# Two parallel branches on one core: the keys' weights turned by DMA in two halves from two queues, the first token tiles on one queue, and a new order of steps

## The chip, the cores and the metric

The kernel runs on one core of a Trainium2 chip. The metric is the device time of one execution in microseconds. The core has a TensorE (PE) for matmuls, a VectorE (DVE), a ScalarE (ACT), a GpSimd (POOL) and a SyncE (SP); each works through its own instructions in their order. DMAs are issued here from SP and from ACT, so a DMA that ACT issues stands in one queue with ACT's arithmetic.

## The reference

x has 2048 tokens of 512 numbers, all in bf16. Both branches read the same normalised tokens; A is a linear attention with 32 heads of 16, B a dense layer with a mish activation.

```python
xn = _layernorm(x, axis=-1)
return x + _A_ref(xn, A_wqkv, A_w_phi, A_wo) + _B_ref(xn, B_w1, B_b1, B_w2)

# _A_ref: q, k, v from x @ wqkv, 32 heads of 16
pq = jnp.einsum("bhsd,hdf->bhsf", q, w_phi)
pk = jnp.einsum("bhsd,hdf->bhsf", k, w_phi)
phi_q = jnp.concatenate([_softmax(pq, axis=-1), _softmax(-pq, axis=-1)], axis=-1)
phi_k = jnp.concatenate([_softmax(pk, axis=-1), _softmax(-pk, axis=-1)], axis=-1)
kv = jnp.einsum("bhsf,bhsd->bhfd", phi_k, v)
z  = jnp.einsum("bhsf->bhf", phi_k)
num = jnp.einsum("bhqf,bhfd->bhqd", phi_q, kv)
den = jnp.einsum("bhqf,bhf->bhq", phi_q, z)[..., None] + 1e-6
o = num / den                      # then @ wo

# _B_ref: w1 is 512 x 1792, w2 is 1792 x 512
h = jnp.einsum("bsd,df->bsf", x, w1) + b1
sp = jnp.log1p(jnp.exp(-jnp.abs(h))) + jnp.where(h > 0, h, jnp.zeros_like(h))
act = h * jnp.tanh(sp)
return jnp.einsum("bsf,fd->bsd", act, w2)
```

## The kernel before

The tokens lie in 16 tiles of 128 (four groups of four). `STEPS` is a string that lists the steps of the whole kernel in the order in which they are written into the program; `run` (L603) maps each name to a function, and the loop at L623 calls them one by one. Under `manual_schedule` (L128) that order is the order on each engine. The number behind `@` is the PSUM bank (six of them), `v` or `a` at the end puts a copy or an inversion on VectorE or ScalarE. The kernel writes no waits; the tile framework places them from what reads and writes what.

**Ahead of the steps** (L483 to L516) the first loads are issued. SP: token tile 0 (L483), then the transposing DMA of the keys' weights (L143), then tiles 2 and 3 (L489), wv (L490), the first half of w1 (L491), tiles 4 to 7 (L492), the second half of w1 (L493). ACT: wsrc (w_phi, L486), token tile 1 (L487), the bias b1b (L488), and the load of the activation table (L495). TensorE does `WARM` matmuls on constants.

**The keys' weights.** The keys are only used through w_phi, so the product of the two weight matrices is formed once: `load_turned` reads a 512 x 512 part of wqkv transposed into wT (partition = column within a block of 128, then block j, then row). `weights_by_block` (WB, L524) lays w_phi out as a block diagonal Wbd. `fold` (F0, L156) multiplies for one block kt of 128 rows of wqkv the four blocks j: its left operand is `wT[:, j, kt * P : (kt + 1) * P]`, so folds 0 and 1 use rows 0 to 255 and folds 2 and 3 rows 256 to 511. `unfold` (FD, L165) copies each to wkp. The same for the queries is done later (WT, F, FC).

**The first tiles** are normalised one by one: LS (moments, DVE, L170 and L172), RS (the root, POOL, L176 and L177), AZ (L181, DVE), TP (turned by TensorE, L560), TC (copied to xnT, L565). `first_logits` (LP, L209) multiplies tiles 0 and 1 by wkp in one step; L, V and WL (L194) do single tiles, LC and VC (L252, L218) copy them out of PSUM. From tile 4 on, LN does the moments of a group, and AP normalises two tiles and turns them by a transposing DMA from SP (L186). DX and DW load tokens and the weights wo and w2 from SP.

**The rest.** H (L228) and M (L239) are the 56 pieces of B's first layer with the mish. For the eight groups of logits (four of keys, four of queries), E takes the extremes (DVE), X the exponentials (ACT), S the sums (DVE, L305), R and N invert and multiply for keys, A adds up kv on TensorE (L387); KV masks it; W weighs the queries and turns them by DMA (L295); Q is the attention (L418), G copies it out, C divides and turns it by DMA (L458); O is B's second layer (L463), P the projection with wo into the same bank (L470), Y adds the tokens and stores (L477, L478). The last tile is split into 384 and 128 columns (OH, PH, YH).

Of the kernel before, what the change touches and what calls it, by code (L numbers as in the profile page):

```python
# [34 lines left out]
@3; H 23 @1; R 0 0 v; N 0 1; M 21; N 0 0; H 24 @4; M 22; LC 2 3 a; F 0 @5; F 1 @0; E 1 0; E 1 1; M
23; M 24; F 2 @2; E 2 0; E 2 1; FC 0 a; H 25 @3; H 26 @1; FC 1 a; H 27 @4; M 25; M 26; L 3 2 @5; FC
2 a; M 27; V 7 @0; L 3 3 @3; V 11 @1; F 3 @2; L 3 0 @4; LC 3 0 v; LC 3 2 a; L 3 1 @5; A 0 0; X 1 0;
X 1 1; A 0 1; LC 3 3 a; FC 3 v; S 1 0; V 8 @4; LC 3 1 a; VC 7 a; L 4 0 @2; E 3 0; VC 8 a; LC 4 0 a;
L 4 1 @3; LC 4 1 a; L 4 3 @5; VC 11 a; L 4 2 @0; X 2 0; V 9 @4; L 5 0 @2; H 28 @3; H 29 @1; VC 9 a;
LC 4 2 v; M 28; M 29; H 30 @0; H 31 @4; H 32 @3; M 30; H 33 @1; H 34 @0; M 31; M 32; M 33; M 34; H  # L40
35 @4; M 35; H 36 @3; M 36; S 1 1; LC 4 3 a; R 1 0 v; E 3 1; LC 5 0 a; N 1 0; R 1 1 v; H 37 @1; H 38
@0; H 39 @4; H 40 @3; H 41 @5; H 42 @2; S 2 0; A 1 0; M 37; N 1 1; M 38; M 39; M 40; A 1 1; M 41; M
42; X 3 0; L 6 3 @1; L 5 2 @0; V 10 @4; VC 10 a; L 5 1 @3; LC 5 2 a; L 6 0 @5; E 4 0; E 4 1; X 2 1;
S 3 0; V 15 @2; VC 15 a; V 13 @4; VC 13 a; LC 6 0 a; R 2 0 a; S 2 1; DW 3; R 3 0 a; X 3 1; L 6 1 @0;
LC 5 1 a; DW 2; N 3 0; N 2 0; L 5 3 @2; O 0 @4; S 3 1; V 12 @5; V 14 @3; LC 6 1 a; LC 5 3 a; O 1 @0;
L 6 2 @2; R 2 1 a; N 2 1; VC 14 a; LC 6 3 a; VC 12 v; R 3 1 a; N 3 1; X 4 0; A 2 0; S 4 0; LC 6 2 a;
A 2 1; A 3 0; W 4 0 v; X 4 1; H 43 @3; M 43; A 3 1; H 44 @1; H 45 @5; M 44; H 46 @2; M 45; H 47 @3;
M 46; M 47; H 48 @1; KV; H 49 @5; H 50 @2; Q 0 0; M 48; M 49; G 0 0; M 50; H 51 @3; H 52 @1; H 53
@5; S 4 1; W 4 1 v; M 51; M 52; H 54 @2; H 55 @3; Q 0 1; M 53; E 5 0; E 5 1; M 54; E 6 0; L 7 0 @1;
M 55; G 0 1; C 0 a; X 5 0; LC 7 0 a; L 7 1 @5; X 5 1; O 2 @2; O 3 @3; LC 7 1 a; L 7 2 @1; LC 7 2 a;  # L50
S 5 0; Q 1 0; L 7 3 @5; G 1 0; E 6 1; W 5 0 a; P 0; P 1; Y 0; Q 1 1; O 4 @1; G 1 1; LC 7 3 a; O 5
@4; S 5 1; Q 2 0; O 6 @5; C 1 a; P 2; G 2 0; W 5 1 v; Y 1; Q 2 1; P 3; O 7 @0; E 7 0; X 6 0; S 6 0;
G 2 1; Q 3 0; C 2 a; G 3 0; Y 2; Y 3; X 6 1; O 8 @2; Q 3 1; W 6 0 v; E 7 1; S 6 1; P 4; P 5; G 3 1;
C 3 a; Q 4 0; X 7 0; Y 4; W 6 1 v; X 7 1; S 7 0; O 9 @3; O 10 @1; G 4 0; Q 4 1; P 6; P 7; G 4 1; Y
# [8 lines left out]
def kernel(  # L63
# [76 lines left out]
    def load_turned(base_col):  # L140

        wT = lnp.tile([P, 4, 512], BF16, name="wT", tag="xn")
        nc.sync.dma_start_transpose(out=wT[:], in_=A_wqkv[:, base_col : base_col + D])  # L143
        return wT
# [57 lines left out]
    def first_logits(how, *b):  # L202
        for i in range(2):
            pl_of[0, i] = bank(b[i], "pl")[:]
        pairs = [(i, kt) for kt in range(KT) for i in range(2)]
        if how == "t":
            pairs.sort()
        for i, kt in pairs:
            nc.tensor.matmul(  # L209
                pl_of[0, i], lhsT=xnT[:, i, kt, :], rhs=wkp[:, kt, :],  # L210
                start=(kt == 0), stop=(kt == KT - 1),
            )
# [270 lines left out]
    nc.sync.dma_start(x_sb[:, 0, :], x_v[:, 0, :])  # L483
# [172 lines left out]
```

## Time and profile before

| what | us |
|---|---|
| runs: median (lowest to highest) of 3 | 174.08 (173.59 to 174.09) |
| the profiled execution, its own time | 174.0 |
| its span, first to last instruction | 172.3 |
| busy: POOL | 9.4 |
| first fold (L156) starts | 6.65 |
| last matmul ends | 169.65 |
| DMA moved in all | 18.02 MB |

The page gives busy times by engine, the span in 40 slices, DMA queues, the chain of work that ended last (each step is followed back to what released it) and groups of instructions by line; a timeline gives start and length of each instruction, with what ended the idle time before it. Times in it count from the start of the span. A matmul's length includes its way through the array, so that a row of matmuls is best read by their distance: in the chain the 48 of L228 that start at 13.78 us take 10.36 us in all, 0.216 us each, though a single one is shown with 379 ns.

### The profile page before, as it was taken

The page shows a single profiled execution, that of the slowest core. Times are in us where ns is not written, and L with a number is a line of the kernel's source. Part 1 is how long each engine was busy: PE and PEld are TensorE (multiplying, and loading weights), DVE is VectorE, ACT ScalarE, POOL GpSimd, SP SyncE. Part 2 cuts the span into 40 slices and gives each one's busy share as a digit, 9 for nine tenths or more (in the row PEclk, how much of TensorE's full clock was granted, in tenths as well). Part 3 has the DMA queues.
Part 4 walks back from the last instruction along what each step waited for, and adds up shares of the span by engine and source line. Part 5 has one row for each costly group of instructions (what it writes and reads, how often), then busy time and mean ns, then how long its engine had stood idle before and what let it go on. Part 6 is the DMA issues. An engine that isn't in the chain of part 4 may idle for free.

```text
span 172.3 us, 2713 instructions
## 1 busy us (share of the span) xinstructions
PE 168.7 (98%) x1039; PEld 82.4 (48%) x1039; DVE 143.2 (83%) x221; ACT 119.5 (69%) x192; POOL 9.4 (5%) x26
## 2 busy tenths in 40 slices
PE   8999999999999999999999999999999999999993
PEld 2554444444545444454446544444444545445452
DVE  2878998999997999979999999799988996844433
ACT  2446889979899998989999988974063883414200
POOL 4332205000000000000000000000000000000000
PEclk9999999999999999999999999999999999999999
DMA  5999350199930000000000363023974749885641
GB/s 98 269 377 365 82 98 0 37 189 207 366 120 0 0 4 0 0 0 0 4 0 0 64 118 66 12 51 67 150 152 93 150 95 144 172 168 100 173 134 61
DMA packets 44953, 18.02 MB, mean 105 GB/s; under 512 B 37004, under 2 KB 44940, under 8 KB 44940
## 3 DMA queue, kind: packets, MB, share of 16 engines
q1 hardware_dynamic: 44096, 17.60, 44.5%
q10 hardware_dynamic: 844, 0.25, 0.6%
q8 instruction: 8, 0.13, 0.3%
q14 instruction: 5, 0.04, 0.1%
HBM read 6.84 MB, written 2.10 MB: 52 GB/s over the span
## 4 chain that ended last, share of the span: by engine, by line
PE 95%; DMA 3%; SPq 0%; DVE 0%; issue 0%
PE po L463 28%; PE ph L228 28%; PE pl L194 14%; PE po L470 8%; PE pv L194 8%; DMA wT<-in_A_wqkv_dram 3%; PE pnd L418 2%; PE pkv L387 2%; PE pfold L156 1%; PE pwide L194 1%; PE pl L209 1%; PE ptr L560 0%; SPq L483 0%; DVE x_sb L477 0%; PE pb L533 0%
## 5 line engine op out<-in xcount | busy, mean ns | idle before, releaser
L463 PE MATMUL po<-w_sb,acts 128*128 128x512 bf16 (+2 forms) x238 | 50.7, 366 | 0.0
L228 PE MATMUL ph<-xnT,w_sb 128*128 128x512 bf16 x224 | 50.1, 379 | 0.0
L239 ACT ACTIVATE acts<-ph,b1f 128x512 bf16<-128x512 f32 x56 | 37.2, 694 | 4.6 <-PE ph L228 4.4
L305 DVE TENSOR_REDUCE s<-e 128x128 f32<-128x2048 bf16 x16 | 36.4, 2279 | 2.5 <-ACT e L288 2.5
L228 PEld LDWEIGHTS <-w_sb 128*128 128x128 bf16 x224 | 21.7, 98 | 25.5
L463 PEld LDWEIGHTS <-acts 128*128 128x128 bf16 x238 | 22.3, 98 | 24.1
L288 ACT ACTIVATE e<-e 128x2048 bf16<-128x2048 bf16 x16 | 30.3, 1908 | 0.0
L194 PEld LDWEIGHTS <-xnT 128*128 128x128 bf16 x184 | 17.6, 98 | 20.1 <-DMA wv<-in_A_wqkv_dram 0.2
L252 ACT CAST p_sb<-pl 128x512 bf16<-128x512 f32 x27 | 15.4, 587 | 5.5 <-PE pl L194 4.7
L433 ACT COPY ds<-pnd 128x32 f32<-128x32 f32 x16 | 2.9, 183 | 23.5 <-PE pnd L418 23.5
L194 PE MATMUL pv<-wv,xnT 128*128 128x512 bf16 x64 | 16.1, 379 | 0.0
L477 DVE TENSOR_TENSOR x_sb<-po,x_sb 128x512 bf16<-128x512 f32 (+2 forms) x17 | 10.9, 654 | 5.7 <-PE po L470 5.7
L470 PE MATMUL po<-wqk,xnT 128*128 128x512 bf16 (+2 forms) x68 | 15.5, 366 | 0.0
L194 PE MATMUL pl<-wqk,xnT 128*128 128x512 bf16 x64 | 15.3, 379 | 0.0
L170 DVE BATCH_NORM_STATS2 stats<-x_sb 128x6 f32<-128x512 bf16 x16 | 10.1, 679 | 4.3 <-DMA x_sb<-in_A_x_dram 4.3
L263 DVE TENSOR_TENSOR m<-m 128x512 bf16<-128x512 bf16 (+1 forms) x32 | 11.5, 358 | 1.1
L194 PE MATMUL pl<-wkp,xnT 128*128 128x512 bf16 x48 | 11.7, 379 | 0.0
L263 DVE TENSOR_TENSOR m<-p_sb 128x1024 bf16<-128x1024 bf16 x16 | 10.9, 682 | 0.2 <-ACT p_sb L252 0.2
L272 DVE TENSOR_TENSOR e<-p_sb,m 128x2048 bf16<-128x2048 bf16 x8 | 9.8, 1226 | 1.4 <-PE pkv L387 1.1
L272 DVE TENSOR_TENSOR e<-m,p_sb 128x2048 bf16<-128x2048 bf16 x8 | 9.8, 1225 | 0.3
L340 DVE TENSOR_TENSOR e<-e,r 128x2048 bf16<-128x2048 bf16 x8 | 9.6, 1215 | 0.0
L138 ACT ACT_TABLE_LOAD x7 | 9.0, 1283 | 0.1
(62 smaller groups left out, 131.4 us busy)
## 6 DMA issues: line engine op xcount, KB each, us to landing
out_dram<-x_sb SPq DMA_DIRECT2D x15, 128.0 KB, 2.0
w_sb<-in_B_w_dram SPq DMA_DIRECT2D x2, 896.0 KB, 7.8
x_sb<-in_A_x_dram SPq DMA_DIRECT2D x3, 512.0 KB, 10.0
w_sb<-in_B_w_dram SPq DMA_DIRECT2D x2, 640.0 KB, 8.8
wv<-in_A_wqkv_dram SPq DMA_DIRECT2D x1, 512.0 KB, 4.5
wqk<-in_A_wo_dram SPq DMA_DIRECT2D x1, 512.0 KB, 4.6
w_sb<-in_B_w_dram SPq DMA_DIRECT2D x1, 512.0 KB, 9.6
x_sb<-in_A_x_dram SPq DMA_DIRECT2D x1, 256.0 KB, 3.2
```

The lines of the kernel that those rows point to most:

```text
L170: nc.vector.bn_stats(stats[:, i, :], xs[:, i, :])
L194: nc.tensor.matmul(pp, lhsT=xnT[:, t, kt, :], rhs=w[:, kt, :], start=(kt == 0), stop=(kt == KT - 1),)
L228: nc.tensor.matmul(ph_of[u][:], lhsT=w1_sb[:, kt, f * P : (f + 1) * P], rhs=xnT[:, g * TPG : (g + 1) * TPG, kt, :], start=(kt == 0), stop= ...
L239: nc.scalar.activation(acts[:, f, g * 512 : (g + 1) * 512], ph_of.pop(u)[:], ACT.Mish, bias=b1f[:, f : f + 1])
L252: copy(p_of[s][:, i, :], pl_of.pop((s, i)))
L263: nc.vector.tensor_tensor(out=m[:], in0=src[:, :, 0:half], in1=src[:, :, half : 2 * half], op=op)
L272: nc.vector.tensor_tensor(out=e_of[s][:].rearrange("p t j l c -> p (t j) l c")[:, :, pl, :].rearrange("p t (c e o) -> p t c e o", e=8, o=2 ...
L288: nc.scalar.activation(v, v, ACT.Exp)
L305: nc.vector.reduce_sum(t[:], pair(s, k).rearrange("p t j l (c e) -> p (t j l c) e", e=16), axis=AX.X)
L463: nc.tensor.matmul(po_of[t, c.stop][:, c], lhsT=acts[:, f, t * P : (t + 1) * P], rhs=w2_sb[:, f, c], start=(f == 0), stop=False,)
L470: nc.tensor.matmul(po_of[t, c.stop][:, c], lhsT=oT_of[t // 2][:, t % 2 * 4 + j, :], rhs=wo_sb[:, j, c], start=False, stop=(j == 3),)
L477: nc.vector.tensor_tensor(out=y, in0=po_of.pop((t, c.stop))[:, c], in1=y, op=ALU.add)
```

## The change

- `load_turned` takes a queue, a tile and a range of rows. The keys' weights are read in two transposing DMAs into one tile wT: rows 0 to 255 from SP, rows 256 to 511 from ACT. The queries' weights are still read whole, from SP.
- Token tiles 0 and 1 are both loaded from SP, ahead of SP's half; on ACT the second half stands behind wsrc and ahead of b1b.
- Eleven warm-up matmuls instead of twelve.
- `first_logits` takes the blocks kt in the order 2, 3, 0, 1; the folds come in that order too.
- Tiles of sums `s` have six buffers instead of three, `r2` three instead of two, `r` one instead of two; the logarithm is written in place instead of to a tile of its own.
- w2 is loaded in two DMAs (7 and 7 blocks) instead of three.
- The steps stand in another order, with other banks and some copies on the other engine. Among it: all four FD are ACT's; both LS come ahead of both RS, and WB behind AZ 0 and TP 0; DW 3 (wo) stands ahead of AP 3 1 and WT; four R of the keys are VectorE's before and three after.

```diff
-WARM = 12
+WARM = 11
 STEPS = """
-LS 0; RS 0; DX 2; LS 1; WB; RS 1; AZ 0; TP 0 @0; F0 0 @1; F0 1 @2; AZ 1; FD 0 v; TP 1 @3; TC 1 v; LS
-2; PB @4; RS 2; TC 0 a; LS 3; RS 3; FD 1 a; AZ 2; F0 2 @5; F0 3 @0; FD 2 a; FD 3 a; LP i @1,2; KM;
-DX 3; AZ 3; V 0 @3; LC 0 0 a; TP 2 @5; V 1 @0; TC 2 a; TP 3 @1; VC 0 a; LC 0 1 v; TC 3 v; CB; L 0 2
-@5; L 0 3 @2; LC 0 3 a; LN 1; H 0 @3; H 1 @1; H 2 @4; M 0; LC 0 2 a; H 3 @2; M 1; M 2; M 3; VC 1 a;
-E 0 0; H 4 @3; H 5 @5; AP 1 0; H 6 @1; H 7 @4; M 4; H 8 @2; M 5; H 9 @0; M 6; M 7; H 10 @3; M 8; M
-9; M 10; AP 1 1; H 11 @5; E 0 1; V 4 @1; X 0 1; WL 1; LN 2; V 6 @4; VC 4 a; X 0 0; L 1 0 @2; L 1 3
-@0; LC 1 0 a; V 5 @3; LN 3; VC 5 a; H 12 @1; WL 2; H 13 @2; VC 6 a; S 0 0; LC 1 3 a; M 11; V 3 @3; M
-12; M 13; H 14 @4; H 15 @0; H 16 @5; H 17 @1; VC 3 a; M 14; H 18 @2; M 15; M 16; M 17; LC 1 2 a; H
...
-0; O 13 @0; Q 6 1; G 6 1; W 7 1 v; P 8; P 9; Q 7 0; C 6 a; G 7 0; P 10; P 11; Y 8; Q 7 1; G 7 1; O
-14 @2; Y 9; Y 10; C 7 a; P 12; P 13; OH 0 @3; PH 0; Y 11; P 14; OH 1 @1; PH 1; Y 12; Y 13; YH 0; Y
-14; YH 1
+LS 0; LS 1; RS 0; RS 1; AZ 0; TP 0 @0; WB; F0 2 @1; F0 3 @2; AZ 1; FD 2 a; TP 1 @3; F0 0 @4; F0 1
+@5; FD 3 a; TC 0 v; TC 1 v; FD 0 a; FD 1 a; LP j @0,1; KM; PB @3; LS 2; RS 2; LS 3; RS 3; CB; DX 2;
+AZ 2; AZ 3; V 1 @2; TP 2 @4; V 0 @5; VC 1 v; TP 3 @3; LC 0 0 a; LC 0 1 a; TC 3 v; TC 2 a; L 0 2 @0;
+LC 0 2 a; H 0 @1; M 0; L 0 3 @4; LC 0 3 a; LN 1; H 1 @2; H 2 @3; E 0 0; VC 0 a; H 3 @0; H 4 @1; H 5
+@4; M 1; AP 1 0; AP 1 1; DX 3; M 2; M 3; H 6 @5; E 0 1; LN 2; M 4; M 5; H 7 @2; H 8 @3; H 9 @0; M 6;
+M 7; M 8; X 0 0; V 2 @1; H 10 @4; S 0 0; L 1 0 @5; LC 1 0 v; V 4 @2; X 0 1; LN 3; VC 2 a; WL 1; H 11
+@3; WL 2; VC 4 a; H 12 @1; H 13 @2; M 9; M 10; R 0 0 v; M 11; M 12; AP 2 0; M 13; AP 2 1; AP 3 0; DW
+3; AP 3 1; WT; H 14 @5; M 14; H 15 @0; L 1 3 @4; LC 1 3 a; LC 1 1 a; LC 1 2 a; E 1 0; S 0 1; E 1 1;
+M 15; H 16 @3; H 17 @1; M 16; M 17; H 18 @2; M 18; H 19 @5; H 20 @4; H 21 @0; H 22 @3; H 23 @1; H 24
+@2; M 19; M 20; H 25 @5; M 21; M 22; H 26 @4; M 23; M 24; H 27 @0; M 25; H 28 @3; N 0 0; H 29 @1; M
+26; M 27; H 30 @2; R 0 1 v; L 2 2 @5; M 28; M 29; M 30; X 1 0; V 3 @4; VC 3 v; L 2 0 @0; L 3 0 @3;
+LC 3 0 a; LC 2 0 a; LC 2 2 a; A 0 0; L 2 3 @1; LC 2 3 a; L 2 1 @2; N 0 1; F 0 @4; F 1 @3; LC 2 1 a;
+F 2 @0; S 1 0; E 2 0; A 0 1; FC 2 a; FC 1 a; F 3 @5; V 6 @1; FC 0 a; FC 3 a; V 10 @2; X 1 1; VC 6 a;
+V 11 @0; V 7 @3; VC 7 a; E 2 1; L 4 0 @4; VC 11 a; L 3 3 @5; L 3 2 @1; V 5 @3; VC 10 a; LC 3 2 v; H
+31 @0; R 1 0 a; VC 5 a; X 2 0; S 1 1; LC 3 3 a; LC 4 0 a; L 4 1 @2; LC 4 1 v; R 1 1 a; L 3 1 @1; LC
...
+0; Q 4 1; X 7 0; O 9 @4; X 7 1; S 6 1; W 6 1 v; G 4 1; Y 5; O 10 @2; O 11 @1; Q 5 0; S 7 0; C 4 a; W
+7 0 a; P 6; P 7; G 5 0; Y 6; S 7 1; Q 5 1; G 5 1; O 12 @0; Q 6 0; C 5 a; W 7 1 v; Y 7; G 6 0; P 8; P
+9; Y 8; Q 6 1; O 13 @5; G 6 1; Q 7 0; P 10; C 6 v; P 11; Y 9; Y 10; G 7 0; Q 7 1; G 7 1; C 7 a; O 14
+@3; P 12; P 13; Y 11; OH 0 @4; PH 0; P 14; OH 1 @2; Y 12; Y 13; YH 0; Y 14; PH 1; YH 1
...
@@ -137,11 +136,8 @@
             tables[0] = name
             nc.scalar.preload_act_table_set(name)
 
-    def load_turned(base_col):
-
-        wT = lnp.tile([P, 4, 512], BF16, name="wT", tag="xn")
-        nc.sync.dma_start_transpose(out=wT[:], in_=A_wqkv[:, base_col : base_col + D])
-        return wT
+    def load_turned(queue, wT, r, base_col):
+        queue.dma_start_transpose(out=wT[:, :, r], in_=A_wqkv[r, base_col : base_col + D])
 
     def bank(b, name, dtype=FP32):
 
@@ -202,13 +198,15 @@
     def first_logits(how, *b):
         for i in range(2):
             pl_of[0, i] = bank(b[i], "pl")[:]
-        pairs = [(i, kt) for kt in range(KT) for i in range(2)]
-        if how == "t":
-            pairs.sort()
+        kts = (2, 3, 0, 1)
+        if how == "j":
+            pairs = [(i, kt) for kt in kts for i in range(2)]
+        else:
+            pairs = [(i, kt) for i in range(2) for kt in kts]
         for i, kt in pairs:
             nc.tensor.matmul(
                 pl_of[0, i], lhsT=xnT[:, i, kt, :], rhs=wkp[:, kt, :],
-                start=(kt == 0), stop=(kt == KT - 1),
+                start=(kt == kts[0]), stop=(kt == kts[-1]),
             )
 
     def value(t, b):
@@ -301,7 +299,7 @@
 
     def sums(s, k):
 
-        t = s_of[s, k] = smx.tile([P, 128], FP32, name="s", bufs=3)
+        t = s_of[s, k] = smx.tile([P, 128], FP32, name="s", bufs=6)
         nc.vector.reduce_sum(
             t[:], pair(s, k).rearrange("p t j l (c e) -> p (t j l c) e", e=16), axis=AX.X
         )
@@ -315,21 +313,20 @@
             out, src.rearrange("p (c o) -> p c o", o=1).to_broadcast([P, n, 2]), ACT.Exp, scale=scale
         )
 
-    def log(src, n):
+    def log(v):
 
         table("natural_log_exp_and_others")
-        t = smx.tile([P, 128], FP32, name="log")
-        nc.scalar.activation(t[:, 0:n], src, ACT.Ln)
-        return t[:, 0:n]
+        nc.scalar.activation(v, v, ACT.Ln)
+        return v
 
     def invert(s, k, how):
 
         t = s_of.pop((s, k))
-        r2 = r_of[s, k] = smx.tile([P, 128, 2], BF16, name="r2")
+        r2 = r_of[s, k] = smx.tile([P, 128, 2], BF16, name="r2", bufs=3)
         if how == "a":
-            power(r2[:], log(t[:], 128), 128, -1.0)
+            power(r2[:], log(t[:]), 128, -1.0)
             return
-        r = smx.tile([P, 128], BF16, name="r")
+        r = smx.tile([P, 128], BF16, name="r", bufs=1)
         with nc.allow_low_precision("the softmaxes are bf16"):
             nc.vector.reciprocal(r[:], t[:])
         nc.vector.tensor_copy(r2[:], r[:].rearrange("p (c o) -> p c o", o=1).to_broadcast([P, 128, 2]))
@@ -348,7 +345,7 @@
         q = smx.tile([P, 16, 4], FP32, name="q")
         r2 = smx.tile([P, 16, 4, 2], BF16, name="q2")
         if how == "a":
-            t4 = log(t[:], 128).rearrange("p (t l c) -> p t l c", l=2, c=4)
+            t4 = log(t[:]).rearrange("p (t l c) -> p t l c", l=2, c=4)
             nc.vector.tensor_tensor(
                 out=q[:], in0=t4[:, :, 0, :], in1=t4[:, :, 1, :], op=ALU.subtract
             )
@@ -444,7 +441,7 @@
         f = opool.tile([P, 64, 2], BF16, name="f")
         d = ds[:].rearrange("p i j c -> p (i j c)")
         if how == "a":
-            power(f[:], log(d, 64), 64, -1.0)
+            power(f[:], log(d), 64, -1.0)
         else:
             w = opool.tile([P, 64], FP32, name="w")
             nc.vector.reciprocal(w[:], d)
@@ -480,11 +477,14 @@
 
     part = (slice(0, 384), slice(384, 512))
 
-    nc.sync.dma_start(x_sb[:, 0, :], x_v[:, 0, :])
-    wT_of = {0: load_turned(D)}
+    for t in range(2):
+        nc.sync.dma_start(x_sb[:, t, :], x_v[:, t, :])
     with nc.allow_non_contiguous_dma(reason="tiny w_phi load"):
         nc.scalar.dma_start(wsrc[:], wphi_v)
-    nc.scalar.dma_start(x_sb[:, 1, :], x_v[:, 1, :])
+
+    wT_of = {0: lnp.tile([P, 4, 512], BF16, name="wT", tag="xn")}
+    load_turned(nc.sync, wT_of[0], slice(0, 256), D)
+    load_turned(nc.scalar, wT_of[0], slice(256, 512), D)
     nc.scalar.dma_start(b1b[:], b1_v[:, :])
     nc.sync.dma_start(x_sb[:, 2:4, :], x_v[:, 2:4, :])
     nc.sync.dma_start(wv[:], wqkv_v[:, :, 2 * D : 3 * D])
@@ -585,7 +585,7 @@
 
     def load_weights(i):
         if i == 2:
-            for f in (slice(0, 5), slice(5, 10), slice(10, FT)):
+            for f in (slice(0, 7), slice(7, FT)):
                 nc.sync.dma_start(w2_sb[:, f, :], w2_v[:, f, :])
         else:
             nc.sync.dma_start(wo_sb, wo_v[:, :, :])
@@ -598,7 +598,8 @@
         pl_of[1, i] = project(wkp, TPG + i, wide_of[0][:, i - 1, :])
 
     def load_queries():
-        wT_of[1] = load_turned(0)
+        wT_of[1] = lnp.tile([P, 4, 512], BF16, name="wT", tag="xn")
+        load_turned(nc.sync, wT_of[1], slice(0, D), 0)
 
     run = {
         "KM": masks, "WB": weights_by_block, "PB": bias,
```

More of the change, by code (lines that the diff above doesn't have):

```diff
@@ L30 @@
-9; M 10; AP 1 1; H 11 @5; E 0 1; V 4 @1; X 0 1; WL 1; LN 2; V 6 @4; VC 4 a; X 0 0; L 1 0 @2; L 1 3
-@0; LC 1 0 a; V 5 @3; LN 3; VC 5 a; H 12 @1; WL 2; H 13 @2; VC 6 a; S 0 0; LC 1 3 a; M 11; V 3 @3; M
-12; M 13; H 14 @4; H 15 @0; H 16 @5; H 17 @1; VC 3 a; M 14; H 18 @2; M 15; M 16; M 17; LC 1 2 a; H
-19 @3; AP 2 0; AP 2 1; AP 3 0; L 2 0 @4; LC 2 0 a; L 2 1 @0; LC 2 1 a; V 2 @5; S 0 1; L 2 2 @1; M
-18; LC 1 1 a; M 19; H 20 @4; LC 2 2 a; AP 3 1; H 21 @0; WT; H 22 @2; M 20; VC 2 a; R 0 1 v; L 2 3
@@ L35 @@
[L35 to L54, printed above, removed]
@@ L55 @@
-5; Y 6; C 4 a; Q 5 0; W 7 0 a; G 5 0; O 11 @4; Q 5 1; Y 7; O 12 @5; S 7 1; G 5 1; C 5 a; Q 6 0; G 6
-0; O 13 @0; Q 6 1; G 6 1; W 7 1 v; P 8; P 9; Q 7 0; C 6 a; G 7 0; P 10; P 11; Y 8; Q 7 1; G 7 1; O
-14 @2; Y 9; Y 10; C 7 a; P 12; P 13; OH 0 @3; PH 0; Y 11; P 14; OH 1 @1; PH 1; Y 12; Y 13; YH 0; Y
-14; YH 1
+LS 0; LS 1; RS 0; RS 1; AZ 0; TP 0 @0; WB; F0 2 @1; F0 3 @2; AZ 1; FD 2 a; TP 1 @3; F0 0 @4; F0 1
+@5; FD 3 a; TC 0 v; TC 1 v; FD 0 a; FD 1 a; LP j @0,1; KM; PB @3; LS 2; RS 2; LS 3; RS 3; CB; DX 2;
@@ new lines @@
+F 2 @0; S 1 0; E 2 0; A 0 1; FC 2 a; FC 1 a; F 3 @5; V 6 @1; FC 0 a; FC 3 a; V 10 @2; X 1 1; VC 6 a;
+V 11 @0; V 7 @3; VC 7 a; E 2 1; L 4 0 @4; VC 11 a; L 3 3 @5; L 3 2 @1; V 5 @3; VC 10 a; LC 3 2 v; H
+31 @0; R 1 0 a; VC 5 a; X 2 0; S 1 1; LC 3 3 a; LC 4 0 a; L 4 1 @2; LC 4 1 v; R 1 1 a; L 3 1 @1; LC
+3 1 v; H 32 @3; H 33 @2; H 34 @5; H 35 @1; L 4 3 @4; M 31; M 32; M 33; M 34; H 36 @0; M 35; M 36; H
+37 @3; M 37; H 38 @2; M 38; H 39 @5; H 40 @1; H 41 @0; H 42 @3; M 39; M 40; H 43 @2; S 2 0; N 1 0; L
@@ new lines @@
+4 2 @5; R 2 0 v; E 3 0; M 41; N 1 1; H 44 @1; M 42; M 43; H 45 @0; A 1 0; LC 4 3 a; A 1 1; E 3 1; LC
+4 2 a; E 4 0; E 4 1; V 9 @3; M 44; V 15 @2; M 45; X 2 1; S 2 1; V 8 @4; VC 8 a; L 6 0 @5; X 3 1; L 5
+0 @1; DW 2; N 2 0; O 0 @0; LC 6 0 a; X 3 0; S 3 0; VC 9 a; S 3 1; L 6 1 @4; VC 15 a; LC 5 0 a; V 14
+@5; VC 14 a; L 5 1 @3; H 46 @2; L 5 3 @1; LC 5 1 a; O 1 @5; LC 6 1 a; R 3 0 a; N 3 0; R 2 1 a; LC 5
+3 a; V 12 @3; L 5 2 @4; V 13 @1; N 2 1; X 4 1; S 4 1; VC 12 a; A 2 0; R 3 1 a; L 6 3 @3; A 2 1; LC 5
@@ new lines @@
+2 a; VC 13 a; L 6 2 @4; A 3 0; X 4 0; LC 6 3 a; N 3 1; A 3 1; H 47 @1; LC 6 2 a; M 46; E 5 0; M 47;
+H 48 @3; H 49 @4; H 50 @2; M 48; H 51 @1; M 49; M 50; S 4 0; M 51; KV; W 4 0 v; E 5 1; H 52 @3; M
+52; H 53 @4; H 54 @2; H 55 @1; W 4 1 v; O 2 @3; Q 0 0; M 53; M 54; E 6 0; M 55; X 5 0; S 5 0; L 7 0
+@4; LC 7 0 a; L 7 1 @2; L 7 3 @1; G 0 0; Q 0 1; G 0 1; O 3 @4; LC 7 1 a; C 0 a; X 5 1; LC 7 3 v; Q 1
+0; O 4 @2; W 5 0 v; G 1 0; E 6 1; S 5 1; L 7 2 @1; LC 7 2 a; Q 1 1; G 1 1; C 1 a; P 0; Y 0; P 1; O 5
@@ new lines @@
+@1; X 6 0; X 6 1; Q 2 0; O 6 @0; W 5 1 v; G 2 0; S 6 0; Y 1; W 6 0 v; Q 2 1; G 2 1; C 2 a; P 2; Y 2;
+P 3; Q 3 0; G 3 0; O 7 @5; Q 3 1; O 8 @3; G 3 1; Q 4 0; E 7 0; P 4; P 5; E 7 1; Y 3; Y 4; C 3 a; G 4
+0; Q 4 1; X 7 0; O 9 @4; X 7 1; S 6 1; W 6 1 v; G 4 1; Y 5; O 10 @2; O 11 @1; Q 5 0; S 7 0; C 4 a; W
+7 0 a; P 6; P 7; G 5 0; Y 6; S 7 1; Q 5 1; G 5 1; O 12 @0; Q 6 0; C 5 a; W 7 1 v; Y 7; G 6 0; P 8; P
+9; Y 8; Q 6 1; O 13 @5; G 6 1; Q 7 0; P 10; C 6 v; P 11; Y 9; Y 10; G 7 0; Q 7 1; G 7 1; C 7 a; O 14
```

## The prediction

> I forecast **slower: 177.8 us**, because the second half of the turned weights will have to wait for the first.
>
> **What bounds the kernel now.** I read the page's busy times first.
>
> ```profile
> PE 168.7 (98%) x1039; PEld 82.4 (48%) x1039; DVE 143.2 (83%) x221; ACT 119.5 (69%) x192; POOL 9.4 (5%) x26
> ```
>
> TensorE leaves nothing to fill; VectorE is next, 25 us behind. Then I read the chain that ended last (start, length, what).
>
> ```profile
> 0.79 0.40 SPq L483
> ...
> 1.25 5.36 DMA wT<-in_A_wqkv_dram
> 6.61 0.05 issue
> 6.65 0.62 PE pfold L156 x8
> 7.27 0.22 PE ptr L560 x4
> ...
> 7.61 0.55 PE pfold L156 x8
> 8.16 1.73 PE pl L209 x8
> 9.88 0.86 PE pv L194 x4
> ...
> 169.41 0.24 PE po L470 x4
> ```
>
> The time has three parts: up to 6.65 us the transposing DMA of the keys' weights (wT); from 6.65 to 169.65 us TensorE without one foreign piece, 163.0 us; and 2.65 us of last addition and store. So a later wT moves the end by the same amount, while a better order in the middle has no TensorE gap to close. The timeline of the head shows what lies beside wT.
>
> ```profile
> 0.79 0.40 SPq L483 DMA_DIRECT2D x_sb<-in_A_x_dram  x1
> 0.83 5.28 PE L513 MATMUL warm<-const-bfloat16-1.0 128*128 128x512 bf16 x12 [0.83 <-PEq L640]
> 1.25 3.12 SPq L143 DMA_TRANSPOSE wT<-in_A_wqkv_dram  x1
> 4.42 0.56 SPq L489 DMA_DIRECT2D x_sb<-in_A_x_dram  x1
> ...
> 5.24 0.41 DVE L524 TENSOR_TENSOR Wbd<-block,wsrc 128x512 bf16<-128x512 bf16 x1
> ...
> 7.31 1.74 ACT L165 CAST wkp<-pfold 128x512 bf16<-128x512 f32 x3
> ```
>
> SP is busy issuing wT until 4.37 us, and the bulk loads start only then; the twelve warm-ups end at about 6.0 us, just before the weights are there. Last, the DMA issues (count, us to landing):
>
> ```profile
> qT<-e SPq DMA_TRANSPOSE x16, 3.2
> xnT<-xn SPq DMA_TRANSPOSE x6, 3.3
> wT<-in_A_wqkv_dram SPq DMA_TRANSPOSE x2, 5.2
> ```
>
> A qT or xnT transpose moves 128x1024 bf16, 256 KB, exactly half of wT's 512 KB. So a half costs 3.2 to 3.3 us and the whole 5.0 (the second wT, with nothing beside it) to 5.36 (the first): about 1.8 us for each 256 KB and 1.4 us that doesn't scale. And all 32 transposes are issued from SP; none shows what two queues do.
>
> **The two halves.** SP now issues two token tiles (0.79 and about 1.24, 0.40 us each) and then its half at about 1.69 instead of 1.25. That half lands 3.3 us later at best, at 5.0; I take 5.2, because the first wT was 0.36 slower than the quiet one. ACT could issue its half at 1.28, behind wsrc, in the slot of today's L487. But the kernel writes no wait by hand: the tile framework places them, and it lets a transpose of one queue start only when an earlier one (in program order) of another queue has landed in full. The ACT half is written second, so it stands on ACT's queue until 5.2 and is issued at about 5.25.
>
> The Trainium skill ("DMA: Bandwidth & Descriptors", Silent corruption: two transposing streams in flight at once) says as much of the chip: the later stream's first transpose must wait for the earlier stream's full count, else both outputs can be spoilt. No run here shows such damage; by that rule the trace has to show the two halves one behind the other.
>
> What does the ACT half cost from 5.25? By then SP, free 1.5 us earlier than today (half of the 3.12 us of issue), has tiles 2 and 3, wv and the first half of w1 in flight, about 1.7 MB. From 8 us on the DMA engines are full in the windows:
>
> ```profile
> 8.00:9.00 1.00, 1.00 (x8) 0.48 (x6) 0.96 (x4) 1.00 (x2) 0.00 (x0) 1.00 0.97 350
> 9.00:10.00 1.00, 1.00 (x7) 0.45 (x5) 0.77 (x3) 0.34 (x2) 0.91 (x3) 1.00 1.03 389
> ```
>
> (The last two columns are the DMA share and GB/s.) No row shows a transpose beside such a load, so I bound it: below by the undisturbed half, 3.2 us, landing at 8.45; above by the 7.3 us that L492's 512 KB took in this same traffic, landing at 12.55. Between them I take 5.0: a half that gets half of the engines takes as long as a whole one that has them all, and the whole is the nearest row in kind. Landing 10.25, first fold 10.3, against 6.65 now: **+3.65 us**.
>
> Queued behind the waiting transpose on ACT are b1b's load (0.67 us of issue), the table load (1.28) and the copies FD and TC. Half the issue time of wT (1.56) from 5.25, then those two, ends at 8.8, before the first copy has anything to copy, so they cost nothing; with the weights at 8.45 it would be 0.1 us. PB needs b1b only after LP, some 4 us later still.
>
> **From the first fold to the first value.** Before: folds at 6.65, L209 ends at 9.88, 3.23 us. After: four folds and one turn (0.28 each and 0.22) start together, but all four copies FD are ACT's, one behind the other: the first fold's result after some 0.45 us, 4 x 0.58 = 2.32, then L209's last two matmuls, 0.43, and 0.1 of handover: 3.3 us. **+0.1 us.** FD 0 was VectorE's (0.69) and is the price of that; VectorE has TC 0 and TC 1 (0.41 each) instead, done 1.4 us after the folds and hidden under the copies.
>
> **Eleven warm-ups.** One fewer is 0.43 us of TensorE, which ends at 5.6; the first turn follows, and then TensorE stands still until 10.3. Worth nothing on the path; price of the gap below.
>
> **The moved loads.** wo (DW 3) moves from behind WT to between AP 3 0 and AP 3 1: 0.57 us of SP's queue ahead of one xnT transpose and of wT for the queries, which land some 0.6 us later, or up to 4.6 (wo's landing) if they share the engines. WT's folds F 0 to F 3 stand at 45 to 46 us of TensorE's summed work, about 20 us behind the load; tiles 14 and 15, which AP 3 1 turns, are first needed by L 3 3, at 51 us of it. Hidden by the H steps between. w2 in two loads instead of three takes one issue (0.5 us) off SP, with nothing waiting.
>
> **Buffers and order.** Six buffers for sums, three r2 and the logarithm in place remove possible waits; the trace has none of them on the chain. The new order has the same TensorE work (163.2 us by the rows in both). I added up VectorE's and ScalarE's rows in the order of the steps: VectorE has 1.3 us more (151.2 against 149.9), ScalarE 1.6 less. What counts is how far a producer's sum is ahead of TensorE's sum at a handover. Tightest now, where TensorE doesn't wait, is V 8 after LC 3 0 on VectorE, 1.0 us; N 1 1 before A 1 1, 1.7. After, N before A never has under 2.3; H 14 behind LC 1 0, which is VectorE's now, is 0.2 short by the sums, but TensorE's sum starts 1 to 2 us later in the span there than VectorE's. I take 0, from 0 to +0.5. At the end, Q 7 1, O 14, P 12, P 13 and the split last tile come in the same sequence: from the Q to PH 0 7.0 us of TensorE cover the gather, the combine (1.4) and the transpose (3.3). 0.
>
> **Sum:** 3.65 + 0.1 + 0 = 3.75 us on the profiled execution's 174.0 (its span 172.3 plus 1.7 outside; the median of the runs is 174.08): **177.8**. With the bounds of the ACT half: 175.9 to 180.1.
>
> **Rivals.**
> *No wait is placed and both halves fly together* (the other side). For it: nothing in the diff is a wait, the halves are disjoint in wT, and the new step order folds 2 and 3, ACT's rows, first. Against: the framework's rule, and that two halves on the same engines need 3.6 us of transfer either way. If each lands 3.3 us after its issue (4.6 and 5.0), the path is x_sb 0's moments, AZ 0 and the blocks (WB) to 5.9; folds at 5.95, copies to 8.7, LP to 9.2 against 9.88: -0.65, 173.35. If they share the engines, they land at 6.3 to 6.6 and it is 174.0. It decides if ACT's half is issued before 5 us.
> *The ACT half is not slowed by the loads:* landing 8.45, 1.85 + 0.1 us, 175.9. For it: its packets have a queue of their own. Against: the share of 1.0.
> *TensorE loses its speed in the gap.* The warm-ups stood 0.43 us apart where the same shape later stands 0.216 apart, for 5.2 us at least, though the granted clock reads 1.00 there. If 4.5 us without work (5.8 to 10.3) brings that back, 5.2 us at half speed lose 2.6, less what the copies hide: about 180. Against: no gap in this trace is long enough to show it. The Trainium skill ("TensorE: Matmul & The Clock Gate", The two states you'll see) lets the clock fall to half after an idle window of about 3.4 us in a free-running grid; the gap can hold such a window or miss it, and no row here shows which.
>
> **How the numbers follow.** The forecast 50%, the unslowed half 17%, the slow clock 15%, no wait and faster 12%, no wait or full cover and no change 6%. The range of 175.2 to 181.0 takes in the bounds of the ACT half and part of the slow clock's cost, and leaves out mainly the 18% of no wait. Slower 82%, same 6% (within 0.3%, 0.5 us, about what such runs can tell from no change), faster 12%.
>
> **What would show it.** ACT's transpose issued only when SP's has landed, near 5.2 us; first fold near 10; TensorE idle for some 4.5 us before it and gapless behind it; the chain of waits with two wT pieces one behind the other. I am wrong if ACT's transpose is issued near 1.3 us, if the folds start before 7 us, or if TensorE has gaps past 15 us. A first fold at 8.5 or 12 leaves the mechanism right and mis-sizes one term.

## The result, and the profile after

The changed kernel takes 176.11 us (median of 6 runs, 175.72 to 177.2) against 173.81 (173.59 to 174.09, 6 runs) for the kernel before beside it: a ratio of 1.0141, 95% interval 1.0106 to 1.0175. Slower, by 2.3 us. The profiled execution took 176.38 us with a span of 174.7 (before: 174.0 and 172.3). In the changed kernel's lines L140 is `load_turned`, L152 `fold`, L161 `unfold`, L190 a product such as the first value, and L207 `first_logits`. First the page's busy times:

```profile
PE 167.5 (96%) x1038; PEld 82.1 (47%) x1038; DVE 144.5 (83%) x224; ACT 118.5 (68%) x188; POOL 9.4 (5%) x26
```

TensorE is busy 1.2 us less, which comes from the warm-ups (eleven in 3.85 us here, twelve in 5.28 before), and the span is 2.4 us longer. Its missing time sits in the head, as the chain that ended last shows (start, length, what):

```profile
1.28 4.02 DMA wT<-in_A_wqkv_dram
5.30 0.02 issue
5.32 1.32 SPq L140
6.64 0.05 issue
6.69 0.57 SPq L489
7.26 0.05 issue
7.31 4.76 DMA wv<-in_A_wqkv_dram
12.07 0.04 issue
12.11 1.02 PE pv L190 x4
```

Before, the chain went through one wT transfer into the folds. Now it goes through one half of wT, then through SP's issue of the other half and of tiles 2 and 3, to the load of wv: the end waits for a plain load that stands on SP's queue **behind the waiting half**. The timeline shows which half that is:

```profile
1.28 1.30 ACTq L140 DMA_TRANSPOSE wT<-in_A_wqkv_dram  x1
...
5.32 1.32 SPq L140 DMA_TRANSPOSE wT<-in_A_wqkv_dram  x1
...
8.76 0.62 PE L152 MATMUL pfold<-Wbd,wT 128*128 128x128 bf16 x8 [1.53 <-DMA wT<-in_A_wqkv_dram]
...
12.11 1.02 PE L190 MATMUL pv<-wv,xnT 128*128 128x512 bf16 x4 [0.90 <-DMA wv<-in_A_wqkv_dram]
```

ACT's half, written second, goes first; SP's half waits. Among SP's waits there is one that the kernel before has nothing like (total, times, longest in us):

```profile
SPq L140 <- DMA wT<-in_A_wqkv_dram: 3.6, 1, 3.6
```

TensorE stands still twice, 1.53 us for SP's half and 0.90 us for wv. Folds 2 and 3 start 0.72 us earlier than any fold before (5.93 against 6.65), but all folds are done only at 9.38 (before 8.16), and the first value comes at 12.11 (before 9.88). The last matmul ends at 172.04 instead of 169.65, 2.39 us later, which is nearly the whole loss. Three questions follow. Is it the split alone, or the new order too? What share has the late half, and what share the loads behind it? And what would the arrangement that the prediction assumed have cost?

### The profile page after: what moved, and what is told of

Read it like the earlier page. It is cut to its first block, busy times and chain, and to the rows that moved or that the text cites. A ratio compares the mean times of both kernels' runs of the same rounds, so it can differ in the third digit from the quotient of the medians.

```text
span 174.7 us, 2707 instructions
## 1 busy us (share of the span) xinstructions
PE 167.5 (96%) x1038; PEld 82.1 (47%) x1038; DVE 144.5 (83%) x224; ACT 118.5 (68%) x188; POOL 9.4 (5%) x26
## 4 chain that ended last, share of the span: by engine, by line
PE 92%; DMA 5%; SPq 1%; ACTq 0%; DVE 0%; issue 0%
PE po L460 28%; PE ph L226 28%; PE pl L190 14%; PE pv L190 8%; PE po L467 8%; DMA wv<-in_A_wqkv_dram 3%; PE pnd L415 2%; PE pkv L384 2%; DMA wT<-in_A_wqkv_dram 2%; PE pwide L190 1%; SPq L140 1%; PE pfold L152 1%; SPq L489 0%; ACTq L483 0%; PE ptr L560 0%; DVE x_sb L474 0%
## 5 line engine op out<-in xcount | busy, mean ns | idle before, releaser
L237 ACT ACTIVATE acts<-ph,b1f 128x512 bf16<-128x512 f32 x56 | 36.3, 702 | 4.9 <-PE ph L226 4.5
L190 PEld LDWEIGHTS <-xnT 128*128 128x128 bf16 x184 | 17.5, 98 | 20.5 <-issue 0.9
L474 DVE TENSOR_TENSOR x_sb<-po,x_sb 128x512 bf16<-128x512 f32 (+2 forms) x17 | 11.1, 655 | 8.1 <-PE po L467 8.1
L250 ACT CAST p_sb<-pl 128x512 bf16<-128x512 f32 x25 | 13.7, 590 | 5.9 <-PE pl L190 5.2
L190 PE MATMUL pv<-wv,xnT 128*128 128x512 bf16 x64 | 15.6, 379 | 0.9 <-DMA wv<-in_A_wqkv_dram 0.9
L166 DVE BATCH_NORM_STATS2 stats<-x_sb 128x6 f32<-128x512 bf16 x16 | 10.1, 680 | 7.2 <-DMA x_sb<-in_A_x_dram 7.2
L190 PE MATMUL pl<-wqk,xnT 128*128 128x512 bf16 x64 | 15.9, 379 | 0.0
L190 PE MATMUL pl<-wkp,xnT 128*128 128x512 bf16 x48 | 11.8, 379 | 0.0
L216 ACT CAST vext<-pv 128x512 bf16<-128x512 f32 x14 | 7.7, 599 | 2.3 <-PE pv L190 2.3
```

The lines of the kernel that those rows point to most:

```text
L166: nc.vector.bn_stats(stats[:, i, :], xs[:, i, :])
L190: nc.tensor.matmul(pp, lhsT=xnT[:, t, kt, :], rhs=w[:, kt, :], start=(kt == 0), stop=(kt == KT - 1),)
L237: nc.scalar.activation(acts[:, f, g * 512 : (g + 1) * 512], ph_of.pop(u)[:], ACT.Mish, bias=b1f[:, f : f + 1])
L250: copy(p_of[s][:, i, :], pl_of.pop((s, i)))
L474: nc.vector.tensor_tensor(out=y, in0=po_of.pop((t, c.stop))[:, c], in1=y, op=ALU.add)
```

## The experiments

The kernel before took 173.76 us beside whole_sp, halves_sp, act_waits and loads_first, 173.88 beside before_split, no_loads_behind, act_quiet and t_first, and 173.88 beside the last three.

**The split undone** (whole_sp): the changed kernel with wT read whole, from SP.

```diff
-    load_turned(nc.sync, wT_of[0], slice(0, 256), D)
-    load_turned(nc.scalar, wT_of[0], slice(256, 512), D)
+    load_turned(nc.sync, wT_of[0], slice(0, D), D)
```

> The changed kernel with the keys' weights read whole by one transposing DMA on SP, as before the change; order, buffers, warm-ups and both first tiles on SP stay as changed. Theory (the cost is the wait between the two queues): no wait; the whole lands about 5.4 us after its issue at 1.7, at 7.1; first fold 7.1, first logits end near 10.4 against 9.88 in the kernel before, wv lands by 10.1: about +0.5 us, 174.3. Rival (the new order, banks or warm-ups cost it): the loss stays, 176.1, with TensorE gaps past 15 us.

Measured: 174.16 us, ratio 1.0019 [1.001, 1.0029]. Its chain:

```profile
1.71 4.89 DMA wT<-in_A_wqkv_dram
6.60 0.04 issue
6.64 0.62 PE pfold L152 x8
...
9.88 0.97 PE pv L190 x4
```

The folds start at 6.64 and the first value at 9.88, as in the kernel before. So the new order, the buffers, both tiles on SP and eleven warm-ups together cost at most 0.3%, and the split makes the loss.

**Two halves on one queue** (halves_sp): what is left of the split without a second queue.

```diff
+    load_turned(nc.sync, wT_of[0], slice(256, 512), D)
     load_turned(nc.sync, wT_of[0], slice(0, 256), D)
-    load_turned(nc.scalar, wT_of[0], slice(256, 512), D)
```

> The changed kernel with both halves on SP, rows 256 to 511 first, one behind the other; all else as changed. Theory: no wait between queues; halves issued at 1.7 and 3.0, landing near 5.2 and 6.9; folds 2 and 3 near 6.0, folds 0 and 1 near 7.0, first logits end near 9.2, wv lands near 9.5, so the first value starts 0.3 us earlier than before: 173.5. Rival (two halves as such cost more than one whole, on whatever queue): second half past 8 us and 174.8 or more. Rival (the order costs it): 176.1.

Measured: 174.44 us, ratio 1.0041 [1.0027, 1.0055]. The expected gain isn't there. On one queue nothing waits: the halves are issued at 1.71 and 3.07 and land at 6.3 and 7.45. But the second lands 0.85 us later than the whole did (6.60), and wv, issued at 5.04, needs 5.18 us and holds the first value back to 10.26. Against whole_sp the split without the wait costs 0.3 us (174.44 against 174.16); with the wait it costs about 2 (176.11).

**The arrangement that the prediction assumed** (act_waits): token tile 1 goes back to ACT's queue ahead of its half, so that SP's half comes first and ACT's half is the one that waits. The rows are exchanged too, so that the half that lands first is still the one that is folded first.

```diff
-    for t in range(2):
-        nc.sync.dma_start(x_sb[:, t, :], x_v[:, t, :])
+    nc.sync.dma_start(x_sb[:, 0, :], x_v[:, 0, :])
...
+    nc.scalar.dma_start(x_sb[:, 1, :], x_v[:, 1, :])
...
-    load_turned(nc.sync, wT_of[0], slice(0, 256), D)
-    load_turned(nc.scalar, wT_of[0], slice(256, 512), D)
+    load_turned(nc.sync, wT_of[0], slice(256, 512), D)
+    load_turned(nc.scalar, wT_of[0], slice(0, 256), D)
```

> The changed kernel with the wait turned round: tile 1 is back on ACT ahead of ACT's half, so SP's half (rows 256 to 511, which the folds take first) stands earlier and ACT's half (rows 0 to 255) is the one that waits. SP's bulk loads then have nothing to wait for. This is the arrangement that the prediction had assumed. SP's half lands near 5.0, ACT's is issued then. Theory (of the measured loss some 1.1 us is the late half and 1.3 us the bulk loads behind SP's wait): wv lands before 9 us and is off the path; ACT's half lands at 8.7 if the loads beside it don't slow it (first logits end 10.9, +1.0 us, 174.9), at 10.0 to 10.3 by the prediction's 5.0 us (first logits end 12.2, +2.3, 176.2). Rival (the loads behind the wait cost nothing): 176.1 with the half landing before 9.

Measured: 184.32 us, ratio 1.0613 [1.0588, 1.0639], far outside every expectation. SP's half lands at 6.10; from there the chain goes:

```profile
6.12 9.67 DMA wT<-in_A_wqkv_dram
15.79 0.05 issue
15.84 1.03 PE pfold L152 x8
16.87 3.15 PE pl L207 x8
```

ACT's half waits, as the prediction had it, and then takes **9.67 us** beside SP's bulk loads. And eight matmuls of the folds take 1.03 us instead of 0.62, those of L207 3.15 instead of 1.73. The windows show why: each line is a stretch, its length, busy time of PE, PEld, DVE, ACT and POOL with counts, granted clock, DMA share and GB/s.

```profile
9.00:11.00 2.00, 0.00 (x0) 0.00 (x0) 0.98 (x4) 1.68 (x3) 1.49 (x4) 0.59 1.08 364
11.00:13.00 2.00, 0.00 (x0) 0.00 (x0) 0.00 (x0) 0.00 (x0) 0.07 (x1) 0.50 1.11 373
19.00:20.00 1.00, 1.00 (x5) 0.20 (x2) 0.00 (x0) 0.16 (x1) 0.00 (x0) 0.69 0.00 0
```

TensorE has nothing to do from about 7.8 to 15.8 us; the granted clock falls to 0.50 and comes back only at about 19.6 us, 3.8 us after the work has. The DMA engines move some 370 GB/s meanwhile, and the loads beside the half lose far less than it does: issue to landing, tiles 4 to 7 took 8.1 us here (before 7.3) and the second half of w1 10.1 (9.2). wv and tiles 2 and 3, in flight mostly beside SP's half, took 5.1 (4.5) and 4.2 (3.2).

**The same in the old order** (before_split): the kernel before with the split alone, ACT's half waiting.

```diff
...
-        nc.sync.dma_start_transpose(out=wT[:], in_=A_wqkv[:, base_col : base_col + D])
+        queue.dma_start_transpose(out=wT[:, :, r], in_=A_wqkv[r, base_col : base_col + D])
...
-    wT_of = {0: load_turned(D)}
+    wT_of = {0: lnp.tile([P, 4, 512], BF16, name="wT", tag="xn")}
+    load_turned(nc.sync, wT_of[0], slice(0, 256), D)
...
+    load_turned(nc.scalar, wT_of[0], slice(256, 512), D)
...
```

> The kernel before with one edit: the weights in two halves, rows 0 to 255 from SP and 256 to 511 from ACT, where ACT's half stands behind wsrc and tile 1. Order, buffers and warm-ups are those of before. ACT's half has to wait for SP's, with SP's bulk loads in flight. Theory (a transpose beside the bulk loads takes 9 to 10 us, and TensorE's clock falls to half in the gap, whatever the order of the steps): SP's half lands near 6, ACT's near 15.5, time near 184. Rival (what act_waits showed belongs to the new order): under 180.

Measured: 185.24 us, ratio 1.067 [1.064, 1.07]. SP's half is issued at 1.24 and lands at 5.23; ACT's half is issued at 5.26 and lands at 16.4, 11.1 us later. TensorE then waits a little longer for b1b, 3.5 KB that ACT issues behind its half at 6.79 and that land at 16.78. So the slow half comes in the old order too.

**Loads ahead of the wait** (loads_first): tiles 2 and 3 and wv are issued from SP ahead of its half, so that nothing the head needs stands behind the wait.

```diff
+    nc.sync.dma_start(x_sb[:, 2:4, :], x_v[:, 2:4, :])
+    nc.sync.dma_start(wv[:], wqkv_v[:, :, 2 * D : 3 * D])
     load_turned(nc.sync, wT_of[0], slice(0, 256), D)
...
-    nc.sync.dma_start(x_sb[:, 2:4, :], x_v[:, 2:4, :])
-    nc.sync.dma_start(wv[:], wqkv_v[:, :, 2 * D : 3 * D])
```

> The changed kernel with tiles 2 and 3 and wv issued from SP ahead of SP's half instead of behind it; the wait on SP stays, and w1 and the later loads still stand behind it. Theory: wv and the tiles land before 8 us, so the wait for wv at 12.1 us is gone and what is left is the late half: landing 8.7 if ACT's half is not slowed by the loads, folds 0 and 1 at 8.8, first logits end 10.95, +1.1 us, 174.9; up to +2.3 if both halves are slowed by 0.6 each. Rival (the loss is the late half alone, not the loads behind it): 176.1 with the half landing before 9.

Measured: 180.14 us, ratio 1.0373 [1.0356, 1.0389].

```profile
1.27 7.29 DMA wT<-in_A_wqkv_dram
...
8.58 3.30 DMA wT<-in_A_wqkv_dram
```

The 768 KB beside ACT's half stretch it from 4.0 to 7.29 us, SP's half starts that much later, and the clock falls again (0.50 from 10 to 12 us). SP's half, with no bulk load in flight on the other queue, takes 3.30. The loads suffer as well, as their issues show (the last column is us from issue to landing):

```profile
wv<-in_A_wqkv_dram SPq DMA_DIRECT2D x1, 512.0 KB, 7.7
x_sb<-in_A_x_dram SPq DMA_DIRECT2D x1, 256.0 KB, 6.7
```

wv, issued at 2.17, takes 7.7 us instead of 4.5 and lands at about 9.9; tiles 2 and 3 take 6.7 instead of 3.2. Both land before they are needed here, since the folds come later still.

**No loads behind the wait** (no_loads_behind): wv and tiles 2 and 3 are not loaded but set to 0.5 on VectorE, so the output isn't the reference's.

```diff
-    nc.sync.dma_start(x_sb[:, 2:4, :], x_v[:, 2:4, :])
-    nc.sync.dma_start(wv[:], wqkv_v[:, :, 2 * D : 3 * D])
+    nc.vector.memset(wv[:], 0.5)
+    nc.vector.memset(x_sb[:, 2:4, :], 0.5)
```

> The changed kernel, but wv and the token tiles 2 and 3 are not loaded: VectorE fills them with 0.5 at the start. So what stands behind SP's wait and is needed early is gone, while the wait and the late second half stay. Theory (of the measured 2.4 us the late half is 1.1 and the loads issued behind the wait, first wv, then tiles 2 and 3, are 1.3): first logits end near 10.95, the first value follows without a gap, 1.1 us behind the kernel before: 174.9. Rival (the late half alone makes the loss): 176.1. Rival (the loads alone make it): 173.8.

```profile
5.15 3.37 DMA wT<-in_A_wqkv_dram
...
8.56 0.62 PE pfold L152 x8
...
11.02 0.97 PE pv L190 x4
```

In this chain (its fold and first value are shown with the transfer before them) the late half is the only thing left: the second pair of folds starts at 8.56 (before 7.61) and the first value at 11.02 (before 9.88), with no wait for wv. (The first pair starts later than in the changed kernel, at 6.71 instead of 5.93, behind VectorE's fillings; that costs nothing, since the second pair waits for the half.) The last matmul ends at 170.89. So of the 2.39 us between 169.65 and 172.04, 1.24 are the late half and **1.15 the loads behind the wait**. The runs fell into two groups, three of 175.37 to 175.68 us with a mean granted clock of 1.0 or 0.998 and three of 176.84 to 177.23 with 0.99; the median of 176.26 (ratio 1.0137 [1.0101, 1.0173]) lies between them, and the split of the loss rests on the traces alone. It is no finer than the spread of the runs: the changed kernel's trace is of an execution of 176.38 us, while its six runs with a clock of 0.999 or 1.0 (here and in after_again) have a median of 176.06; against the 175.38 of the first group that makes the loads worth 0.7 us instead of 1.15.

**Is it ACT's queue, the wait, or the traffic?** (act_quiet): as act_waits, but the five bulk loads (and a later token load, DX 2) stand on ACT's own queue, behind its half.

```diff
...
-    load_turned(nc.sync, wT_of[0], slice(0, 256), D)
-    load_turned(nc.scalar, wT_of[0], slice(256, 512), D)
+    load_turned(nc.sync, wT_of[0], slice(256, 512), D)
...
+    load_turned(nc.scalar, wT_of[0], slice(0, 256), D)
+    nc.scalar.dma_start(x_sb[:, 2:4, :], x_v[:, 2:4, :])
+    nc.scalar.dma_start(wv[:], wqkv_v[:, :, 2 * D : 3 * D])
...
-        nc.sync.dma_start(
+        (nc.scalar if g == 2 else nc.sync).dma_start(
```

> act_waits with the bulk loads taken from SP and put behind ACT's half on ACT's own queue (b1b and the table load ahead of it, DX 2 on ACT too), so that ACT's half waits as in act_waits but has nothing beside it. Theory (the loads in flight on the other queue slow it): it lands 3.3 to 3.5 us after its issue near 5, at 8.4, and the time is near 176. Rival (a transpose from ACT, or one that has waited, is slow in itself): 9 to 10 us again, and 183 or more.

Measured: 178.44 us, ratio 1.0261 [1.0235, 1.0286]. ACT's half is issued at 5.15 behind the wait. The timeline shows the folds that need it:

```profile
8.57 0.62 PE L152 MATMUL pfold<-Wbd,wT 128*128 128x128 bf16 x8 [1.47 <-DMA wT<-in_A_wqkv_dram]
```

The same half from the same queue after the same wait lands in 3.4 us when the loads stand behind it on its own queue instead of flying from the other one. The other queue's traffic makes the 9.67, not ACT's queue and not the wait; this rests on one trace. The time (two runs) misses its expectation by over 2 us, since ACT's copies stand behind the loads' issues and the clock falls again:

```profile
11.00:12.00 1.00, 1.00 (x4) 0.36 (x3) 0.93 (x4) 0.52 (x2) 0.50 (x2) 0.50 1.04 384
```

**The transpose first** (t_first): wT whole, as SP's first DMA; tiles 0 and 1 on ACT ahead of wsrc.

```diff
+    wT_of = {0: lnp.tile([P, 4, 512], BF16, name="wT", tag="xn")}
+    load_turned(nc.sync, wT_of[0], slice(0, D), D)
...
-        nc.sync.dma_start(x_sb[:, t, :], x_v[:, t, :])
+        nc.scalar.dma_start(x_sb[:, t, :], x_v[:, t, :])
...
```

> The changed kernel with the weights read whole by SP, as SP's first DMA at 0.8 us; tiles 0 and 1 go to ACT ahead of wsrc. Nothing else stands in flight with it but those 256 KB. Theory (a transposing DMA that is issued early and has little beside it lands early, and the loads behind it on the same queue come early too): weights land near 6.2, folds at 6.2 to 6.4, first logits end near 9.4, wv lands by 9.4, so the first value starts some 0.4 us earlier than in the kernel before: 173.4. Rival (the tiles' 256 KB on the other queue slow the transpose, as 768 KB did in loads_first): landing at 7 or later, 174.2 or more.

```profile
1.20 4.46 DMA x_sb<-in_A_x_dram
```

Measured: 175.17 us, ratio 1.0086 [1.0058, 1.0114]; a miss, and the line of its chain shows why. The 128 KB of token tile 1, issued behind the transpose, take 4.46 us (3.1 in the kernel before), and VectorE has its moments ahead of AZ 0, so the first value comes at 10.88.

**The same, less exposed** (t_first2): tile 0 before tile 1 on VectorE, the folds ahead of the second turn, L207 tile by tile.

```diff
-LS 0; LS 1; RS 0; RS 1; AZ 0; TP 0 @0; WB; F0 2 @1; F0 3 @2; AZ 1; FD 2 a; TP 1 @3; F0 0 @4; F0 1
-@5; FD 3 a; TC 0 v; TC 1 v; FD 0 a; FD 1 a; LP j @0,1; KM; PB @3; LS 2; RS 2; LS 3; RS 3; CB; DX 2;
+LS 0; RS 0; WB; AZ 0; TP 0 @0; LS 1; RS 1; F0 2 @1; F0 3 @2; F0 0 @4; F0 1 @5; FD 2 a; TC 0 v; AZ 1;
+TP 1 @3; FD 3 a; FD 0 a; TC 1 v; FD 1 a; LP i @0,1; KM; PB @3; LS 2; RS 2; LS 3; RS 3; CB; DX 2;
```

> t_first with the moments of tile 0, its root, the blocks and its normalising ahead of tile 1 on VectorE, all four folds ahead of the second turn, and the first logits tile by tile. In t_first tile 1 landed 4.5 us after its issue, beside the transpose, and tile 0's normalising stood behind it. Theory (what t_first lost, it lost to tile 1 being late and first in line): weights at 6.4, folds done by 7.5, the copies by 9.2, first value near 9.6 against 9.88 in the kernel before, time near 173.5. Rival (tile 1's late landing holds the second half of the first logits just as long): first value past 9.9 and 173.9 or more.

Measured: 177.4 us, the median of five runs of 176.53 to 178.53 (a sixth took 179.62), 1.02 times the kernel before; a worse miss. Now wsrc's 16 KB, behind both tiles on ACT's queue, are late, 4.68 us after their issue (before 2.5), so the block diagonal is formed at 6.46 and the first turn starts at 7.26. TensorE stands still from 4.81 to 7.26, and after it the window from 8 to 9 us reads a clock of 0.50, after a gap of only 2.45 us.

**The changed kernel again, and with its gaps filled** (after_again, after_filled). The second writes seven matmuls on constants ahead of folds 0 and 1 and four ahead of the first value.

```diff
-LS 0; LS 1; RS 0; RS 1; AZ 0; TP 0 @0; WB; F0 2 @1; F0 3 @2; AZ 1; FD 2 a; TP 1 @3; F0 0 @4; F0 1
-@5; FD 3 a; TC 0 v; TC 1 v; FD 0 a; FD 1 a; LP j @0,1; KM; PB @3; LS 2; RS 2; LS 3; RS 3; CB; DX 2;
+LS 0; LS 1; RS 0; RS 1; AZ 0; TP 0 @0; WB; F0 2 @1; F0 3 @2; AZ 1; FD 2 a; TP 1 @3; WF 7 4; F0 0 @4; F0 1
+@5; FD 3 a; TC 0 v; TC 1 v; FD 0 a; FD 1 a; LP j @0,1; KM; PB @3; WF 4 2; LS 2; RS 2; LS 3; RS 3; CB; DX 2;
...
```

> The changed kernel once more, for a second profile and more times beside their granted clock. So far three of its runs stand at 175.7 to 175.8 with a mean clock of 1.0, two at 176.9 and 177.2 with 0.99. Theory (waiting in the head makes 2.0 us, and a clock that falls to half for a stretch in some executions makes another 1.1 to 1.5): again two clusters, which go with the clock. Rival (the spread is that of landing times): times between 175.7 and 177.2 whatever the clock.

> The changed kernel with matmuls on constants in the two gaps of TensorE: seven ahead of the folds 0 and 1, four ahead of the first value; they fill 1.5 and 0.9 us in which TensorE would wait anyway. Theory (the gaps let the clock fall in some executions): all runs at a mean clock of 1.0 and near 175.8, the cluster near 177 gone. Rival (the clock has nothing to do with the gaps): the same two clusters as the changed kernel. Late landings as such stay as they are, so nothing under 175.5 in either case.

Measured: 176.8 us (176.28 to 176.98), ratio 1.0164 [1.0149, 1.0178], and 176.59 (176.48 to 176.72), ratio 1.0157 [1.0144, 1.017]. Over the ten runs of the changed kernel, the four with a mean clock of 0.99 took 176.87 to 177.2 us, and the six with 1.0 or 0.999 took 175.72 to 176.72. With the gaps filled none of four runs reads 0.99, as expected, but none is at 175.8 either; its first value came at 12.42 in the trace. Four runs can't show that the filling removed the 0.99; the spread at full clock stays unexplained.

## Why the prediction was right, and where it was wrong

**Slower because one half waits for the other:** right. The halves went one behind the other with no wait written in the diff, as the chain shows, and whole_sp brings the time back.

**Which half waits:** wrong; this is the step that failed: "The ACT half is written second, so it stands on ACT's queue until 5.2". The half that stands second on its queue (ACT, behind wsrc) went before the half that stands third on its own (SP, behind two tiles). In act_waits, before_split and act_quiet SP's half is second on its queue and goes first; in loads_first SP's half is fifth and waits. That the position in the queues decides fits all of them, and so does that the half goes first whose queue is free first; it is read from the traces, neither was tried by itself, and only the order in which the halves are written is ruled out. With it fell the first fold near 10.3: the prediction's own signs for being wrong, ACT's transpose near 1.3 us and folds before 7, both came.

**The second half at 5.0 us (3.2 to 7.3), +3.65:** mis-sized in both directions. In the kernel as changed it waits on SP, so SP's loads wait with it and it runs nearly alone: 3.4 us (5.32 to 8.72). In the arrangement that I had priced it took 9.67 and 11.1, above my upper bound. That bound was a plain load in the same traffic; the transpose fared worse there (256 KB in 9.67 us, against 8.1 for the 512 KB of tiles 4 to 7 in act_waits). The row that the 5.0 us comes from, the second wT of the kernel before, did not have "nothing beside it" either: it is issued at 38.04 us, right behind the transposes of xn (issued until 37.87), and the load of wo follows at 39.91.

**What is queued behind the waiting instruction:** I looked at ACT's queue, where nothing was urgent. The wait sat on SP's, and wv stood behind it: issued at 7.31 instead of 5.04, landed at 12.07. That term, 1.15 us, is missing in the sum. The late half makes 1.24 of the 2.39 instead of 3.75 of 3.75. So the sum was 1.4 us too high on the profiled execution (177.8 against 176.38), with one term too large and one left out. That the measured time lies so near is in part luck: the two mistakes are of opposite sign, and the arrangement that was priced costs 184.32.

**The rivals.** The unslowed half, 175.9, came nearest in number, and rightly in the duration of the half, but on the other queue and without the loads. Both halves flying together didn't happen; its point of decision, ACT's half issued before 5 us, was badly chosen, since that half may go first while the other waits. The slow clock was shown for a gap of 8 us (act_waits), and it came after gaps of 2.45 (t_first2) and 1.47 and 0.91 (act_quiet) too. In the changed kernel's profiled execution it played no part (0.999); in the runs with 0.99 it goes with about 1 us, which no trace of such a run shows in place.

**The terms of nothing** held: order, buffers, moved loads and warm-ups by whole_sp, where first fold to first value is 3.24 us against 3.23, so that my +0.1 was not there either. From the first value on the chain is gapless in both kernels: the 2.23 us at the first value (12.11 against 9.88) become 2.39 at the last matmul.

## What to carry to other kernels

Before a transfer is split over two queues, ask whether the two parts may run together; if not, the split adds a wait, and its price is the late part and what stands behind it on that queue. The half that is written second need not be the one that waits: read from the trace which one does, and look in the chain for a load whose issue was late rather than whose transfer was long. Keep a transposing DMA that the head waits for away from bulk loads of the other queue: both lose, and in act_waits the transpose lost most.
